# A two-layer GELU network on one core: the order of the first loads and the dummy matmuls around the first turns

## The chip, the core and the metric

The kernel runs on one core of a Trainium2 chip. The metric is the device time of one execution in microseconds; the times shown are the median of several runs.

The engines that matter here are TensorE (PE in the profile, with its weight loads PEld apart), VectorE (DVE), ScalarE (ACT), GpSimd (POOL) and SyncE (SP). Each runs its own list of instructions in order and meets the others at semaphores. SyncE, ScalarE and GpSimd also issue DMA transfers; issues appear as SPq, ACTq and POOLq.

## The reference

```python
B, S, D, F = 1, 2048, 448, 1792      # x, w1, b1, w2, b2 all bf16

def reference(x, w1, b1, w2, b2):
    h = jnp.einsum("bsd,df->bsf", x, w1) + b1
    h = _gelu(h)                      # tanh approximation
    return jnp.einsum("bsf,fd->bsd", h, w2) + b2
```

## The kernel before

The 2048 rows of x go through in four chunks of 512. For each chunk layer 1 makes h transposed (14 tiles of 128 features, by 512 rows), ScalarE applies bias and GELU on the way from PSUM to SBUF (line 284), and layer 2 multiplies by w2 and adds b2. The contraction of layer 1 is 448 long: three blocks of 128 and one of 64. Every matmul uses 64 of the array's 128 rows; matmuls come in pairs, one on each half of the rows, writing two PSUM banks, and go together. All layer matmuls are issued through `mm`, so they share line 226.

Layer 1 is written as objects `Layer1(c, j)`, j from 0 to 6, each for two feature tiles. `a` is the first half of the rows' work over the three blocks, `b_main` the second, `b_last` the 64-long rest and the activations. For the first chunk the order is by hand: the first 256 rows of x for object 0 (`L[0].a(0, HC)`), then its second 256 rows, then object 1, and so on.

x must be transposed before layer 1 can use it. For chunks 1 to 3 a DMA does it (line 151). For the first chunk TensorE does it: x's first 512 rows are loaded as they are, in two halves of 256 rows (`load_x`, line 156, events x 0 and x 1), and "turned" by transposing matmuls (`turn`, line 353): twelve for the first half, twelve for the second, and later four for the 64-wide rest (`turn_rest`). VectorE and ScalarE drain the turned blocks from PSUM (lines 364 and 366, events xT0, half, block).

Ahead of the turns TensorE runs dummies, matmuls of constant ones whose results nobody reads (`warm`, line 201): six of 512 columns and one of 128 before the first turns, one of 128 between the first and the second.

w1 is loaded in five pieces by feature tiles, cut at 0, 2, 4, 8, 12 and 14 (`load_w1`, line 134): piece 0 holds the two tiles of object 0 and has 192 KB, piece 1 those of object 1, 192 KB too, piece 2 the four tiles of objects 2 and 3. Their events are w1 0, w1 1 and so on. The last 64 rows of w1 are loaded apart in two pieces (`load_w1r`, line 141), and VectorE copies part of them to the other half of the partitions (line 420).

What sets the order of the loads is each issuing engine's list. SyncE issues x's first half, w1 piece 0, then waits at a `barrier` for the event "table", which ScalarE sets after a one-column activation that makes it load its GELU table (line 184); then come all other weights, b2, the transposing loads of x, and the stores. ScalarE issues x's second half and w1 piece 1 right at its start. GpSimd sets up the identity matrix (lines 176 and 177), sets `b2_z` to zero (line 180, event b2z0) and then issues the load of b1. The loads of these pieces have no wait of their own.

A first layer-1 matmul of object 0 waits for w1 piece 0 and for the drained block of x that it reads. A dummy waits for nothing in the kernel before; on TensorE all instructions go in the order of the list.

Of the kernel before, what the change touches and what calls it, by code (L numbers as in the profile page):

```python
# [77 lines left out]
def bass_standalone__dense_activation_gelu__prompt_kernel(  # L78
# [10 lines left out]
    P = 128  # L89
    H = P // 2  # L90
    SC = 512
    HC = SC // 2
# [9 lines left out]
    with ExitStack() as es:  # L102
# [18 lines left out]
        pr = Program(nc, es)  # L121
# [10 lines left out]
        def load_w1(i, engine="sync"):  # L132
            c0, c1 = W1CUTS[i] * P, W1CUTS[i + 1] * P
            pr.dma(engine, lambda e: e.dma_start(
                w1_sb[:, :, c0:c1], w1[0:D3, c0:c1].rearrange("(k p) f -> p k f", p=P)), ("w1", i))
# [3 lines left out]
        def load_w1r(i, engine="sync"):  # L139
            cs = slice(RCUTS[i] * P, RCUTS[i + 1] * P)  # L140
            pr.dma(engine, lambda e: e.dma_start(w1r[H:P, cs], w1[D3:D, cs]), ("w1r", i))
# [13 lines left out]
        def load_x(h, engine):  # L155
            pr.dma(engine, lambda e: e.dma_start(
                xn[:, 2 * h:2 * h + 2, :], x2[h * HC:(h + 1) * HC, :].rearrange("(p t) d -> p t d", t=2)), ("x", h))

        o0v = [out2[h * HC:(h + 1) * HC, :].rearrange("(p t) d -> p t d", t=2) for h in (0, 1)]
        load_x(0, "sync")  # L160
        load_w1(0)
        pr.barrier("sync", ["table"])
        load_w1r(0)
        load_w1(2)
        load_w1r(1)
# [5 lines left out]
        for c in range(1, NSC):  # L171
            for slot in range(KT + 1):
# [10 lines left out]
               after=["b1z"])  # L183
        pr.op("scalar", lambda e: e.activation(junk[:, :], one, ACT.Gelu_apprx_tanh), event="table")  # L184
        load_x(1, "scalar")
        load_w1(1, "scalar")

        def turn_b1():
            for q in range(4):
                pr.op("vector", lambda e, q=q: e.transpose(  # L190
                    b1t[32 * q:32 * q + 32, :], b1n[:, 32 * q:32 * q + 32]), after=["b1n"], event=("b1t", q))
            pr.op("vector", lambda e: e.tensor_copy(b1_f[:, :], b1t[:, 0:NFT]),
                  after=[("b1t", q) for q in range(4)], event="b1")
# [2 lines left out]
            pr.op("vector", lambda e: e.tensor_copy(xT[0:H, KT, s0:s1], xT[H:P, KT, s0:s1]),  # L196
                  after=after, event=event)

        def warm(n, cols=SC, u=0):
            for _ in range(n):  # L200
                pr.op("tensor", lambda e: e.matmul(unit[u][:, 0, 0:cols], lhsT=ones_w, rhs=ones_m[:, 0:cols],  # L201
                                                   start=True, stop=True))

# [150 lines left out]
        def turn_block(h, k, u, i, wait=()):  # L356
            for t in (0, 1):
                turn(lambda half, t=t: spot(u, i)[:, half, t, :], lambda rows, t=t: xn[rows, 2 * h + t, k * P:(k + 1) * P],
                     ("xt", h, k) if t else None, [("x", h)] + list(wait))
# [9 lines left out]
        def drain_block(engine, h, k, u, i, after):  # L369
            move(engine,  # L370
                 lambda t: xT[:, k, h * HC:(h + 1) * HC].bitcast(t).rearrange("p (t b s) -> p b t s", b=2, t=2),
                 lambda t: unit[u][:, :, i * H:(i + 1) * H].bitcast(t).rearrange("p b (t s) -> p b t s", t=2),
                 [after], ("xT0", h, k))
            busy[(u, 0)] = ("xT0", h, k)

        def turn_first():
            for k in (0, 2, 1):
                turn_block(0, k, k, 0)
                drain_block(("vector", "vector", "scalar")[k], 0, k, k, 0, ("xt", 0, k))
            warm(1, P, 3)  # L380
            pr.op("vector", lambda e: e.tensor_copy(
                xr[:, :, :].rearrange("p q (two h) -> p q two h", two=2),
                xn[:, :, D3:D].rearrange("p (q two) h -> p q two h", two=2)), after=[("x", 0), ("x", 1)],
                event="xr_in")
            for k in range(KT):
                turn_block(1, k, 3, k)
            for k in range(KT):
                drain_block("vector", 1, k, 3, k, ("xt", 1, 2))

        def turn_rest():  # L390


            for q in range(STC // 2):
                turn(lambda half, q=q: spot(2, 1)[:, half, q, :], lambda rows, q=q: xr[rows, q, :], ("xr", q),
                     ["xr_in", ("xT0", 0, 2)])
            for src, engine in enumerate(("vector", "scalar")):
                for dst in (src, 1 - src):
                    move(engine,
                         lambda t, src=src, dst=dst: xT[HALVES[dst], KT, 0:SC].bitcast(t).rearrange(
                             "p (q two b s) -> p b q two s", q=2, two=2, b=2)[:, :, :, src, :],  # L400
                         lambda t, src=src: unit[2][HALVES[src], :, H:2 * H].bitcast(t).rearrange(
                             "p b (q s) -> p b q s", q=2),
                         [("xr", 1)], ("xR0", dst, src))
            busy[(2, 1)] = ("xR0", 1, 0)
            busy[(2, 2)] = ("xR0", 0, 1)

        warm(NWARM)
        warm(1, P)
        turn_first()
        L = [Layer1(0, j) for j in range(NPAIR)]  # L410
        L[0].a(0, HC)
        L[0].step("a", 0, HC, SC)
        L[0].step("a", 1, HC, SC)
        turn_rest()
        L[0].step("a", 2, HC, SC)

        for i in (0, 1):
# [3 lines left out]
                  after=[("w1r", i)], event=("w1rU", i))  # L421
            if i == 0:
                turn_b1()
        L[1].a()
        L[0].b_main()
        L[1].b_main()
# [8 lines left out]
        for c in range(NSC):  # L435
# [7 lines left out]
            else:  # L443

                for row in (0, H):
                    pr.op("vector", lambda e, row=row: e.tensor_copy(b2_z[row:row + 1, :], b2_bc[row:row + 1, :]),  # L446
                          after=["b2", "b2z0"], event="b2z" if row else None)
# [59 lines left out]
```

## Time and profile before

| What | Value |
|---|---|
| Median of 5 runs | 94.37 us (93.68, 94.09, 94.37, 95.98, 96.09) |
| The profiled execution | 96.07 us; its span 94.8 us |
| PE busy | 91.5 us, 97% of the span |
| PEld busy | 51.9 us, 55% |
| ACT busy | 38.1 us, 40% |
| DVE busy | 13.8 us, 15% |
| POOL busy | 1.7 us, 2% |
| Issue of x's two halves, w1 pieces 0 and 1 | 0.75, 0.81, 1.20, 1.25 us |
| ScalarE's table ready, first SyncE issue after it | 2.25 us, 2.28 us |
| b2_z on GpSimd | 1.42 to 1.89 us |

Times within the execution are counted from its first instruction. A row of a group names the line, engine, operation, what it writes and reads, the shape and the count. In the order of time the first column is the start and the second the time from the first start to the last end of a merged run of instructions; in brackets stands how long the engine was idle before it, and what was seen to release it. Ends of matmuls are modelled, so their starts, and the starts of the weight loads, tell more than their durations. Rows of DMA issues end with the time from issue to landing.

### The profile page before, as it was taken

To read this page: it belongs to the slowest core of one execution; us is meant where nothing else is said; L and a number is where in the kernel's file an instruction comes from. 1 tells how busy PE (TensorE), PEld (TensorE's weight loads), DVE (VectorE), ACT (ScalarE), POOL (GpSimd) and SP (SyncE) were. 2 spreads that over 40 slices of the span, in tenths; PEclk is the share of its full clock that TensorE was granted. 3 is DMA by queue.
4 is the path that set the end of the run, shared out by engine and by line. 5 is a ranking of instruction groups with operands and counts; after the bars stand their busy time and mean duration, and the time that the engine had idled before them with its cause. 6 is when DMAs were issued, how large, how long until landed. Compare 5 with 4: busy or idle time off the path is not lost.

```text
span 94.8 us, 2059 instructions
## 1 busy us (share of the span) xinstructions
PE 91.5 (97%) x940; PEld 51.9 (55%) x940; DVE 13.8 (15%) x37; ACT 38.1 (40%) x63; POOL 1.7 (2%) x8
## 2 busy tenths in 40 slices
PE   6989999999999999999999999999999999999990
PEld 2464454555555444555555444555554444579990
DVE  0256002100046000000046000000044000000331
ACT  6120597830000788830000878820000878820011
POOL 6000000000000000000000000000000000000000
PEclk9999999999999999999999999999999999999999
DMA  2999999655663100000022100000021100000023
GB/s 79 320 263 330 379 282 121 120 102 111 99 107 112 49 0 7 0 0 0 0 88 64 48 0 0 3 7 0 0 96 67 37 0 0 0 0 7 0 97 97
DMA packets 13544, 7.32 MB, mean 77 GB/s; under 512 B 7264, under 2 KB 13472, under 8 KB 13536
## 3 DMA queue, kind: packets, MB, share of 16 engines
q1 hardware_dynamic: 12688, 6.70, 30.4%
q10 hardware_dynamic: 816, 0.49, 1.7%
q8 instruction: 7, 0.11, 0.5%
q14 instruction: 1, 0.01, 0.0%
q0 software_dynamic: 32, 0.00, 0.0%
HBM read 3.79 MB, written 1.84 MB: 59 GB/s over the span
## 4 chain that ended last, share of the span: by engine, by line
PE 97%; DVE 0%; ACT 0%; issue 0%
PE u L226 92%; PE u L201 3%; PE u L353 1%; DVE xT L366 0%; ACT out_sb L334 0%
## 5 line engine op out<-in xcount | busy, mean ns | idle before, releaser
L284 ACT ACTIVATE g<-u,b_f 128x512 bf16<-128x512 f32 x56 | 34.8, 685 | 41.4 <-PE u L226 41.4
L226 PE MATMUL u<-xT,w_sb 64*128 64x512 bf16 (+1 forms) x342 | 43.4, 390 | 0.4 <-DVE xT L366 0.4
L226 PE MATMUL u<-w_sb,g 64*128 64x448 bf16 (+2 forms) x504 | 43.3, 329 | 0.0
L226 PEld LDWEIGHTS u<-w_sb,g 64*128 64x128 bf16 x504 | 27.7, 94 | 15.2
L226 PEld LDWEIGHTS u<-xT,w_sb 64*128 64x128 bf16 x342 | 19.1, 98 | 19.1 <-issue 1.8
L337 DVE TENSOR_TENSOR out_sb<-u,b_bc 128x448 bf16<-128x448 f32 (+2 forms) x16 | 8.9, 591 | 64.5 <-PE u L226 64.5
L226 PE MATMUL u<-xT,w1r 64*128 64x512 bf16 x56 | 10.7, 376 | 0.0
L226 PEld LDWEIGHTS u<-xT,w1r 64*128 64x128 bf16 x56 | 3.1, 96 | 3.2 <-issue 0.4
L334 ACT CAST out_sb<-u 128x320 bf16<-128x320 f32 (+1 forms) x2 | 0.7, 345 | 8.8 <-PE u L226 8.8
L201 PE MATMUL u<-const-bfloat16-1.0 128*128 128x512 bf16 (+1 forms) x8 | 3.1, 545 | 0.8 <-PEq L492 0.8
L364 ACT COPY xT<-u 64x256 bf16<-64x256 bf16 (+1 forms) x3 | 1.1, 369 | 3.8 <-PE u L353 3.8
L366 DVE TENSOR_SCALAR xT<-u 128x128 uint32<-128x128 uint32 (+1 forms) x7 | 1.8, 285 | 4.2 <-PE u L353 4.2
L201 PEld LDWEIGHTS u<-const-bfloat16-1.0 128*128 128x128 bf16 x8 | 1.0, 134 | 2.2 <-issue 2.1
L184 ACT ACT_TABLE_LOAD x1 | 1.3, 1283 | 0.8 <-PEq L492 0.8
L446 DVE COPY b_z<-b_bc 1x448 bf16<-1x448 bf16 x2 | 0.5, 266 | 5.8 <-DMA b_bc<-in_b_dram 5.8
L196 DVE COPY xT<-xT 64x512 bf16<-64x512 bf16 x3 | 0.9, 288 | 3.1 <-DMA xT<-in_x_dram 3.1
L353 PEld LDWEIGHTS u<-ident,xn 64*128 64x128 bf16 x24 | 0.7, 121 | 0.6 <-DMA xn<-in_x_dram 0.5
L353 PE MATMUL u<-ident,xn 64*128 64x64 bf16 x24 | 1.0, 237 | 0.0
L190 DVE STREAM_TRANSPOSE b1t<-b1n 32x32 bf16<-32x32 bf16 x4 | 0.8, 202 | 0.1
L182 POOL DMA_DIRECT2D b1n<-in_b_dram x1 | 0.6, 647 | 0.0
L420 DVE COPY w1r<-w1r 64x256 bf16<-64x256 bf16 (+1 forms) x2 | 0.6, 289 | 0.4 <-DMA w1r<-in_w_dram 0.4
L180 POOL MEMSET b_z<- 128x448 bf16 x1 | 0.5, 467 | 0.0
(14 smaller groups left out, 2.7 us busy)
## 6 DMA issues: line engine op xcount, KB each, us to landing
w_sb<-in_w_dram SPq DMA_DIRECT2D x2, 784.0 KB, 8.0
out_dram<-out_sb SPq DMA_DIRECT2D x14, 112.0 KB, 1.7
w_sb<-in_w_dram SPq DMA_DIRECT2D x2, 384.0 KB, 5.4
w_sb<-in_w_dram SPq DMA_DIRECT2D x2, 192.0 KB, 4.7
xn<-in_x_dram SPq DMA_DIRECT2D x1, 224.0 KB, 2.5
xn<-in_x_dram ACTq DMA_DIRECT2D x1, 224.0 KB, 3.0
w_sb<-in_w_dram ACTq DMA_DIRECT2D x1, 192.0 KB, 4.1
xT<-in_x_dram SPq DMA_TRANSPOSE x12, 4.3
```

What stands on the lines that cost most here:

```text
L182: pr.dma("gpsimd", lambda e: e.dma_start(b1n[0:NFT, :], b1.rearrange("(c p) -> c p", p=P)), "b1n", after=["b1z"])
L184: pr.op("scalar", lambda e: e.activation(junk[:, :], one, ACT.Gelu_apprx_tanh), event="table")
L190: pr.op("vector", lambda e, q=q: e.transpose(b1t[32 * q:32 * q + 32, :], b1n[:, 32 * q:32 * q + 32]), after=["b1n"], event=("b1t", q))
L196: pr.op("vector", lambda e: e.tensor_copy(xT[0:H, KT, s0:s1], xT[H:P, KT, s0:s1]), after=after, event=event)
L201: pr.op("tensor", lambda e: e.matmul(unit[u][:, 0, 0:cols], lhsT=ones_w, rhs=ones_m[:, 0:cols], start=True, stop=True))
L226: o = pr.op("tensor", lambda e: e.matmul(unit[u][:, lo, cols], lhsT=lhsT, rhs=rhs, start=start, stop=stop, skip_group_check=skip), after=a ...
L284: pr.op("scalar", lambda e, lo=lo, ft=ft: e.activation(g[:, ft, c * SC:(c + 1) * SC], unit[u][:, lo, :], ACT.Gelu_apprx_tanh, bias=b1_f[:, ...
L334: pr.op("scalar", lambda e, j=j: e.copy(out_sb[:, j, d0:d1], unit[u][:, 1, 0:d1 - d0]), after=[("y", j, d0)], event=("o", j, d0))
L337: pr.op("vector", lambda e, j=j, lo=lo: e.tensor_tensor(out=out_sb[:, j, d0:d1], in0=unit[u][:, lo, 0:d1 - d0], in1=b2_bc[:, d0:d1], op=AL ...
L353: pr.op("tensor", lambda e, half=half, rows=rows: e.transpose(o(half), i(rows), ident[rows, rows]), after=after + ["ident"], event=event i ...
L364: pr.op(engine, lambda e: e.copy(out(BF16), in_(BF16)), after=after, event=event)
L366: pr.op(engine, lambda e: e.tensor_single_scalar(out(U32), in_(U32), 0, ALU.bitwise_or), after=after, event=event)
```

## The change

The first pieces of w1 change places: piece 0 is now issued by ScalarE, behind x's second half, and piece 1 by SyncE. SyncE's wait stands ahead of piece 1 now, and is for b2_z's zeros on GpSimd in place of ScalarE's table. The dummy ahead of the first turns and the one between the turns grow from 128 to 256 columns. A third dummy of 256 columns is put behind the second turns; it waits for the first drained block of x, and the layer-1 matmuls come after it. The lists of ScalarE, GpSimd and VectorE are otherwise the same.

```diff
         load_x(0, "sync")
-        load_w1(0)
-        pr.barrier("sync", ["table"])
+        pr.barrier("sync", ["b2z0"])
+        load_w1(1)
         load_w1r(0)
         load_w1(2)
...
         load_x(1, "scalar")
-        load_w1(1, "scalar")
+        load_w1(0, "scalar")
...
-        def warm(n, cols=SC, u=0):
+        def warm(n, cols=SC, u=0, after=()):
             for _ in range(n):
                 pr.op("tensor", lambda e: e.matmul(unit[u][:, 0, 0:cols], lhsT=ones_w, rhs=ones_m[:, 0:cols],
-                                                   start=True, stop=True))
+                                                   start=True, stop=True), after=after)
...
                 turn_block(0, k, k, 0)
                 drain_block(("vector", "vector", "scalar")[k], 0, k, k, 0, ("xt", 0, k))
-            warm(1, P, 3)
+            warm(1, HC, 3)
...
         warm(NWARM)
-        warm(1, P)
+        warm(1, HC)
         turn_first()
+        warm(1, HC, 0, [("xT0", 0, 0)])
         L = [Layer1(0, j) for j in range(NPAIR)]
         L[0].a(0, HC)
```

## The prediction

> **What bounds the kernel now.** I read the chain of waits first. It is TensorE work nearly from end to end:
>
> ```profile
> 4.72 0.02 issue
> 4.74 0.30 DVE xT L366
> 5.04 0.01 issue
> 5.05 1.25 PE u L226 x10
> 6.30 0.11 PE u L353 x4
> 6.41 86.24 PE u L226 x891
> ```
>
> After 5.05 us TensorE never stops, so the end can move only by (a) when that stream starts and (b) how fast its matmuls go. Fewer bytes or faster engines elsewhere are worth nothing.
>
> For (b) I put two stretches of the layer-1 matmuls side by side, 6.3 to 9.7 us and 10.4 to 14 us (columns: count, then minimum/median/maximum ns of one):
>
> ```profile
> L226 PE MATMUL u<-xT,w_sb x19: 398/631/632, 5.9 to 9.4; 64*128 64x512 bf16 x16, 64*128 64x256 bf16 x3
> ...
> L226 PE MATMUL u<-xT,w_sb x30: 376/376/377, 10.6 to 13.8; 64*128 64x512 bf16 x30
> ```
>
> The same form takes 631 ns early and 376 ns late. Those are latencies; the rate is in the weight loads between, from the order of time:
>
> ```profile
> 9.38 0.17 PEld L226 LDWEIGHTS u<-xT,w_sb 64*128 64x128 bf16 x2 [0.25 <-issue]
> 9.81 0.17 PEld L226 LDWEIGHTS u<-xT,w1r 64*128 64x128 bf16 x2 [0.25 <-issue]
> ...
> 10.13 0.11 PEld L226 LDWEIGHTS u<-xT,w1r 64*128 64x128 bf16 x2 [0.15 <-issue]
> 10.35 0.11 PEld L226 LDWEIGHTS u<-xT,w_sb 64*128 64x128 bf16 x2
> ```
>
> A pair of loads serves a pair of 512-column matmuls, one in each half of the rows, that run together. The step is 0.43 us (9.38 to 9.81), then 0.32, then 0.22. So TensorE ran at half rate until W = 10.03 us: the step of 0.32 is 0.22 us at half and 0.10 at full rate, and 9.81 + 0.22 = 10.03. The page's clock row shows 9 tenths all along and can't be used for this. Every us of dense work before W costs half a us.
>
> For (a), the order of time ahead of the stream:
>
> ```profile
> 0.79 2.83 PE L201 MATMUL u<-const-bfloat16-1.0 128*128 128x512 bf16 x7 [0.79 <-PEq L492]
> 3.54 0.50 PE L353 MATMUL u<-ident,xn 64*128 64x64 bf16 x12
> 3.98 0.29 PE L201 MATMUL u<-const-bfloat16-1.0 128*128 128x128 bf16 x1
> 4.20 0.50 PE L353 MATMUL u<-ident,xn 64*128 64x64 bf16 x12
> 5.05 1.25 PE L226 MATMUL u<-xT,w_sb 64*128 64x256 bf16 x10 [0.35 <-DVE xT L366]
> ```
>
> TensorE idles for 0.35 us before the stream. The releaser named, a DVE drain of x's second half, is not needed by the first matmul, whose own drain (the first on DVE, from 3.87) was long done. It also needs w1's first tiles, and these are the late ones:
>
> ```profile
> xn<-in_x_dram SPq DMA_DIRECT2D x1, 224.0 KB, 2.5
> xn<-in_x_dram ACTq DMA_DIRECT2D x1, 224.0 KB, 3.0
> w_sb<-in_w_dram SPq DMA_DIRECT2D x1, 192.0 KB, 3.7
> w_sb<-in_w_dram ACTq DMA_DIRECT2D x1, 192.0 KB, 4.1
> ```
>
> Issued at 0.75, 0.81, 1.20 and 1.25, they land at 3.2, 3.8, 4.9 and 5.3 us.
>
> [...]
>
> [...] The profiled execution took 96.07 us (span 94.8 and 1.27 around it), 1.7 above the median of 94.37. Of the five runs, two (95.98, 96.09) look like the profiled one, and three (93.68, 94.09, 94.37) like runs that switched earlier: (96.07 - 94.37) x 2 = 3.4 us earlier, so at 6.6, and 5.25 for the fastest. These are estimates, since only one trace is there.
>
> **The change, part by part.**
>
> *Longer dummies before and between the turns.* 128 columns more each, at half rate 0.427 x 128 / 512 = 0.107 us each. Neither is covered: x's first half landed at 3.2 and the turns start at 3.54, when the dummies are through; the second landed at 3.8, before the turns at 4.20. So 0.21 us on TensorE's path, less up to 0.03 at the first.
>
> *The new dummy after the turns.* It waits for the first drain on DVE, done by 4.17, before TensorE gets there, so the wait costs nothing. 256 columns are 0.21 us; changing from turns to a dummy and back costs as the middle dummy does: turns through at about 3.86, next at 4.20, that is 0.34 with 0.107 of columns, so 0.23 of change. Sum 0.44 us. Behind it on TensorE stands the whole stream. The second turns, through at about 4.51, are now through at 4.71; plus 0.44 is 5.15. The stream starts at **5.15 for 5.05: +0.10 us**, with the idle 0.35 us as cover for the rest.
>
> *w1's first tiles (event w1 0) on ScalarE's queue.* Issued at 1.25 in place of 1.20, behind x's second half (3.8). *Its next tiles (w1 1)* leave SyncE once b2_z's memset on GpSimd ends (1.42 + 0.47 = 1.89), so about 1.91 in place of 1.25. That takes 192 KB from beside the first tiles for some 0.6 us. At the 309 KB/us and more of 2 to 4 us, the first tiles should land 0.2 to 0.5 us earlier, 4.4 to 4.7; bounds: 4.2 and, if the order in the queue hurts, 5.5. Worth nothing by itself while the dummies run to 5.15, but it makes the start TensorE's own. The next tiles land later, 5.4 to 5.9 for 5.3. They are needed after six pairs of 256 columns and four turns: 6 x 0.21 + 0.1 = 1.4 us past the start at half rate, 0.75 at full rate, so at 5.9 or later: nothing, but nothing to spare.
>
> *All later loads on SyncE.* The old wait ended at 2.25 with the table; now one issue (0.42) and a gap come after 1.91, so the rest is issued 0.15 to 0.2 us later: w1r's first part (landed 5.7; its copy on DVE starts only at 7.08), w1's 384 KB tiles (landed 8.0, to 8.2), all else. In the trace these have slack; at full rate from the start, the 384 KB tiles are wanted after those six pairs and 11 pairs of 512 columns (11 x 0.216 = 2.4), at about 5.15 + 0.75 + 2.4 = 8.3: no loss counted, up to 0.3 us possible. GpSimd and ScalarE issue the same things in the same order: nothing.
>
> [...] TensorE is now busy from 0.79 on but for the changes of mode, with 0.43 us more dummy columns around the turns[...] the fastest run before already suggests 5.25. I take 4.7[...]. Saving (10.03 - 4.7) / 2 = 2.67; cost 0.10, half of it if the clock is up by then: 96.07 - 2.67 + 0.05 = **93.4 us**. Bounds: W at 3.5 gives 92.8; 6.6 gives 94.4.
>
> **Rivals.**
>
> [...] (0.17). Short gaps don't decide, or the dummies are too few. Then the time is the median plus 0.10: 94.5. For it: three runs of five were quick without the change. Against: two were not[...].
>
> *The first tiles come later[...]* (0.23; slower). [...] If they land where the next tiles do now, at 5.33, the stream starts at 5.45: +0.4 us of idle beside the new dummy, which gives back the 0.43 of new columns, so nearly every run switches at about 10: 96.07 + 0.1 to 0.2 = 96.2. It decides from a landing past 5.15. Against it: the next tiles are issued 0.66 us later than the first.
>
> *The hold does nothing*: the next tiles' data begins when it did, since a transfer's data starts well after its issue (nothing moves before 1.8 us). Then landings stay near 4.9, still before 5.15, and the main case holds; its price is none.
>
> **How the numbers follow.** Main case 0.60, its own range 92.7 to 94.4; [...] 0.45 faster by over 1% (below 93.43), 0.15 within. No effect: 0.12 within, 0.03 faster, 0.02 slower. Late tiles: 0.23 slower. One per cent is about what a measurement of this kernel can tell from no change. Faster 0.48, same 0.27, slower 0.25. The range must reach into the slow case: 92.7 to 96.1.
>
> **What would show it.** Right: no idle time before the first L226 matmul, which starts at 5.1 to 5.2; the first tiles landed by 4.7; three L201 dummies of 256 columns; steps of 0.22 us between weight loads from about 5 us. Wrong: W still near 10; or a landing past 5.15 with idle time before the stream. [...]

## The result and the profile after

| | before | changed |
|---|---|---|
| Median of all runs | 94.00 us (93.30 to 96.35, 79 runs) | 94.17 us (93.59 to 96.05, 44 runs) |
| Runs at 95.4 us or more | 29 of 79 | 2 of 44 |
| Mean of all runs | 94.55 us | 94.24 us |
| The other runs: mean, first and last tenth | 93.81; 93.51, 94.17 | 94.16; 93.82, 94.48 |
| Ratio to before | | 1.0037, interval 1.0024 to 1.0050 |

The ratio leaves out runs more than 1.5% above the quickest of their kernel, which here are those in which TensorE's clock rises late (95.4 us or more, the late runs of what follows). So the change is 0.4% slower in the ratio, and it does something else that the ratio can't show: the gap between 94.6 and 95.4, in which no run of this table lies, is crossed by far fewer runs.

The profiled execution of the changed kernel (96.05 us, span 94.7) has the late clock, as that of before had, so the two can be laid side by side. The chain of waits (start, length, what):

```profile
0.74 0.46 ACT L184
1.20 0.03 issue
1.22 4.33 DMA w_sb<-in_w_dram
5.56 0.05 issue
5.61 1.25 PE u L226 x7
6.85 0.11 PE u L353 x4
6.96 85.65 PE u L226 x702
```

Before, the chain ran through TensorE's dummies and turns to a stream that starts at 5.05. Now its head is a transfer: piece 0 of w1, issued by ScalarE at 1.22, which lands 4.33 us later. The stream starts at 5.61. TensorE's own order of time (start, length, engine, line, shape, count, and in brackets the idle time ahead and its releaser):

```profile
3.65 0.50 PE L353 MATMUL u<-ident,xn 64*128 64x64 bf16 x12
4.08 0.40 PE L201 MATMUL u<-const-bfloat16-1.0 128*128 128x256 bf16 x1
4.41 0.50 PE L353 MATMUL u<-ident,xn 64*128 64x64 bf16 x12
4.84 0.40 PE L201 MATMUL u<-const-bfloat16-1.0 128*128 128x256 bf16 x1
5.61 0.39 PE L226 MATMUL u<-xT,w_sb 64*128 64x256 bf16 x2 [0.37 <-DMA w_sb<-in_w_dram]
```

The turns and dummies are where the prediction put them (turns at 3.65 for 3.54 and 4.41 for 4.20, third dummy at 4.84), but 0.37 us of idle time is still there. The issues and their time to landing:

```profile
xn<-in_x_dram SPq DMA_DIRECT2D x1, 224.0 KB, 2.6
xn<-in_x_dram ACTq DMA_DIRECT2D x1, 224.0 KB, 3.0
w_sb<-in_w_dram ACTq DMA_DIRECT2D x1, 192.0 KB, 4.3
w_sb<-in_w_dram SPq DMA_DIRECT2D x1, 192.0 KB, 4.0
```

Piece 0 takes 4.3 us where it took 3.7, and lands at 5.56. Piece 1, issued at 1.91, takes 4.0 and lands at 5.88, where it was at 5.33. The rate, from the weight loads:

```profile
8.68 0.15 PEld L226 LDWEIGHTS u<-xT,w_sb 64*128 64x128 bf16 x2 [0.28 <-issue]
9.10 0.15 PEld L226 LDWEIGHTS u<-xT,w_sb 64*128 64x128 bf16 x2 [0.28 <-issue]
9.47 0.31 PEld L226 LDWEIGHTS u<-xT,w_sb 64*128 64x128 bf16 x4 [0.22 <-issue]
```

The steps are 0.42, then 0.37, after which four loads come in 0.31. The step of 0.37 is 0.30 us at half and 0.07 at full rate, so the clock rises at 9.10 + 0.30 = 9.40 us, against 10.03 before. That gain of 0.63 us is worth 0.31, and the start 0.56 us later, in a stretch at half rate, costs 0.28. The spans are 94.7 and 94.8. Here the two nearly cancel. Most runs of the changed kernel are not like this one, and what sets their time took the experiments to see.

### The profile page after: what moved, and what is told of

Read it like the earlier page. It is cut to its first block, busy times and chain, and to the rows that moved or that the text cites. A ratio compares the mean times of both kernels' runs of the same rounds, so it can differ in the third digit from the quotient of the medians.

```text
span 94.7 us, 2060 instructions
## 1 busy us (share of the span) xinstructions
PE 91.4 (97%) x941; PEld 46.3 (49%) x941; DVE 13.8 (15%) x37; ACT 38.2 (40%) x63; POOL 1.7 (2%) x8
## 4 chain that ended last, share of the span: by engine, by line
PE 92%; DMA 5%; ACT 1%; issue 0%
PE u L226 92%; DMA w_sb<-in_w_dram 5%; ACT L184 0%; ACT out_sb L334 0%; PE u L353 0%
## 5 line engine op out<-in xcount | busy, mean ns | idle before, releaser
L226 PE MATMUL u<-xT,w_sb 64*128 64x512 bf16 (+1 forms) x342 | 42.5, 386 | 0.4 <-DMA w_sb<-in_w_dram 0.4
L226 PEld LDWEIGHTS u<-w_sb,g 64*128 64x128 bf16 x504 | 25.0, 94 | 17.8
L226 PEld LDWEIGHTS u<-xT,w_sb 64*128 64x128 bf16 x342 | 16.5, 97 | 21.5 <-issue 1.6
L201 PE MATMUL u<-const-bfloat16-1.0 128*128 128x512 bf16 (+1 forms) x9 | 3.7, 552 | 0.8 <-PEq L493 0.8
L226 PEld LDWEIGHTS u<-xT,w1r 64*128 64x128 bf16 x56 | 2.6, 94 | 3.4
```

What stands on the lines that cost most here:

```text
L226: o = pr.op("tensor", lambda e: e.matmul(unit[u][:, lo, cols], lhsT=lhsT, rhs=rhs, start=start, stop=stop, skip_group_check=skip), after=a ...
```

## The experiments

**The first four** take the change apart. The theories named in the expectations: A, the order of loads costs and the dummies help the clock; B, the loads cost nothing and the dummies cost; C, the ratio above 1 is only the mix of runs.

The order of loads alone, with the dummies of before:

```diff
         load_x(0, "sync")
-        load_w1(0)
-        pr.barrier("sync", ["table"])
+        pr.barrier("sync", ["b2z0"])
+        load_w1(1)
...
-        load_w1(1, "scalar")
+        load_w1(0, "scalar")
```

> The changed order of loads alone (w1 piece 0 on ScalarE behind x's second half, piece 1 on SyncE behind the zeros), with the dummies of the kernel before. Theory A (the loads cost, the dummies help the clock): the first layer-1 matmul starts up to 0.5 us later than 5.05, and with the idle gap longer the clock rises late (times of 95.4 and more) in as many runs as before or more, over 35%; the other runs are 0.2 to 0.5 us above those of before, ratio 1.003 to 1.005. Theory B (the loads cost nothing, the dummies cost): ratio 0.999 to 1.001.

Measured: ratio 1.0028 (0.9998 to 1.0058), span 93.1; 1 of 14 runs late. The size fits A, though the interval just reaches 1; the place does not fit: piece 0 landed at 4.68 and the stream started at 4.81, earlier than before. The loss is further on:

```profile
4.81 1.25 PE L226 MATMUL u<-xT,w_sb 64*128 64x256 bf16 x10
5.83 0.34 PE L353 MATMUL u<-ident,xr 64*128 64x64 bf16 x4
5.96 0.34 PE L226 MATMUL u<-xT,w_sb 64*128 64x256 bf16 x2
6.57 0.60 PE L226 MATMUL u<-xT,w_sb 64*128 64x512 bf16 x4 [0.27 <-DMA w_sb<-in_w_dram]
```

This is TensorE in order of time. The first object's last pair is at 5.96, and the second object, whose matmuls have 512 columns, starts at 6.57, released by a transfer: piece 1, which landed at 6.53. And the clock rose early nearly always (24 of 67 runs of the kernel before were late beside it), though no dummy was added. With piece 0 there sooner, no idle time is listed ahead of the stream (0.35 us in the profile before); that this is the reason is not shown.

The dummies alone, with the loads of before:

```diff
-            warm(1, P, 3)
+            warm(1, HC, 3)
...
-        warm(1, P)
+        warm(1, HC)
         turn_first()
+        warm(1, HC, 0, [("xT0", 0, 0)])
```

> The three dummies alone, with the order of loads of before. Theory A: the late rise of the clock all but goes (under 10% of the runs at 95.4 or more), the stream starts at 5.15 to 5.2 in place of 5.05, other runs at 93.9 to 94.0, ratio 1.001 to 1.002. Theory B: the ratio is that of the whole change, 1.003 to 1.005. Theory C (the ratio above 1 is only that runs which were late before now sit at the upper end of the quick ones): the quickest tenth is where it was before, 93.5, and the slowest tenth of the quick runs moves from 94.2 to 94.5.

Measured: median 93.81 beside 94.01 of before, ratio 1.0001 (0.9978 to 1.0025), span 92.1; 0 of 22 late. B falls here; a repeat below has 1.0022. The first tenth of the runs is at 93.54 and the last at 94.44, as C has it for these dummies. In the changed kernel C is not enough: there both tenths lie 0.31 us higher than before (93.51 and 94.17, 93.82 and 94.48). The profile has full rate from the start of the stream and no wait at the second object (5.47 is the first object's last pair, the second follows at 5.59):

```profile
4.62 0.28 PE L201 MATMUL u<-const-bfloat16-1.0 128*128 128x256 bf16 x1
4.84 0.72 PE L226 MATMUL u<-xT,w_sb 64*128 64x256 bf16 x10
5.40 0.22 PE L353 MATMUL u<-ident,xr 64*128 64x64 bf16 x4
5.47 1.15 PE L226 MATMUL u<-xT,w_sb 64*128 64x256 bf16 x10
```

All dummies, piece 0 back on SyncE, piece 1 behind the zeros on SyncE too:

```diff
         load_x(0, "sync")
+        load_w1(0)
         pr.barrier("sync", ["b2z0"])
         load_w1(1)
...
-        load_w1(0, "scalar")
```

> All dummies of the change, but w1 piece 0 stays on SyncE right behind x's first half; piece 1 follows on SyncE after the zeros, and ScalarE issues only x's second half. Theory A, if it is the place behind x's second half in ScalarE's queue that delays piece 0: it lands by 4.6, the stream starts at 5.15, ratio 1.000 to 1.002. If it is the late piece 1 and its followers that get in the way, as in the change: 1.003 to 1.005.

Measured: ratio 1.0042 (1.0026 to 1.0058), span 92.8; 0 of 22 late. Piece 0 landed at 4.75 and the stream started at 4.92; piece 1 landed at 6.11. The weight loads show the wait (0.50 us of idle time):

```profile
5.56 0.10 PEld L226 LDWEIGHTS u<-xT,w_sb 64*128 64x128 bf16 x2
6.16 0.33 PEld L226 LDWEIGHTS u<-xT,w_sb 64*128 64x128 bf16 x6 [0.50 <-DMA w_sb<-in_w_dram]
```

So ScalarE's queue is not needed for the loss; the hold of piece 1 is enough.

The change without its third dummy (its line taken out):

> The change without its third dummy. If the third dummy is what the clock needs: late rises come back, over 20% of the runs at 95.4 or more. If it is on the path of the quick runs: these gain 0.1 to 0.3 us over the change, ratio about 1.001; if the landing of w1 piece 0 sets the start anyway, they stay at 94.15, ratio 1.003 to 1.004.

Measured: ratio 1.0024 (1.0005 to 1.0043), span 93.0; 0 of 22 late, though one run, at 95.22, lies between the two groups and is not in the ratio. The late rises did not come back, against what I expected of the third dummy. Piece 0 landed at 4.74, piece 1 at 6.34, and the second object started at 6.39: the quick runs stay where they were (median 94.16).

**The next four** test the hold from the other side, and the dummies.

The change with piece 1 on SyncE right behind x's first half:

```diff
-        pr.barrier("sync", ["b2z0"])
         load_w1(1)
+        pr.barrier("sync", ["table"])
```

> The change without its hold: w1 piece 0 on ScalarE behind x's second half, piece 1 on SyncE right behind x's first half at 1.2 us, SyncE's wait for the table after it as before; all three dummies. If the hold is the cause (piece 1 lands at 6.1 to 6.5 and TensorE waits for it at the second object): piece 1 lands by 5.6, no idle time there, quick runs as with the dummies alone, ratio 0.999 to 1.001. If the place of piece 0 behind x's second half is the cause: piece 0 lands past 5.1, ratio 1.003 or more.

Measured: ratio 1.0047 (1.0029 to 1.0065), span 92.9; 3 of 7 late. The hold is gone, piece 1 landed at 5.08, and it is no better: now piece 0 is the last of the four and landed at 5.56:

```profile
4.65 0.28 PE L201 MATMUL u<-const-bfloat16-1.0 128*128 128x256 bf16 x1
5.61 0.72 PE L226 MATMUL u<-xT,w_sb 64*128 64x256 bf16 x10 [0.67 <-DMA w_sb<-in_w_dram]
```

The idle time ahead of the stream is longer than before (0.67 us for 0.35), and late rises are back in spite of all the dummies, though of seven runs only. My first theory held the hold alone to blame; without it the ratio is no lower (1.0047, and 1.0048 for the change in the same batch), with the wait at piece 0 in place of piece 1.

The two longer dummies without the third, loads of before:

> Loads of the kernel before, the two longer dummies, no third. If length ahead of and between the turns is enough for the clock: under 10% of the runs at 95.4 or more. If the gap after the second turns decides: about as many as before, over 25%. Quick runs 0 to 0.1 us under those with the third, ratio 0.999 to 1.000.

Measured: 4 of 22 late (12 of 30 of the kernel before beside it), ratio 1.0024 (1.0007 to 1.0041), between the two answers that I had given for the late runs; the quick runs are not quicker than with the third dummy.

The change once more, for a profile with the early clock:

> The change once more, for the profile of an execution whose clock rises early. If the wait is for piece 1: the stream starts at 4.8 to 5.0, piece 1 lands at 6.1 to 6.5, TensorE waits for it from about 5.7 and loses 0.4 to 0.7 us there; span 92.6 to 93.0 against 92.1 with the dummies alone; ratio 1.003 to 1.005. If piece 0 is what is late, as in the profile with the late clock: the stream starts past 5.3.

Measured: ratio 1.0048 (1.0030 to 1.0066), span 93.2; 0 of 7 late. Piece 0 landed at 4.69, piece 1 at 6.46. The expected wait is not there:

```profile
5.18 1.25 PE L226 MATMUL u<-xT,w_sb 64*128 64x256 bf16 x10
6.22 0.32 PE L353 MATMUL u<-ident,xr 64*128 64x64 bf16 x4
6.34 0.86 PE L226 MATMUL u<-xT,w_sb 64*128 64x256 bf16 x6
```

In this execution the first object ran at half rate (ten matmuls in 1.25 us, against 0.72 with the dummies alone) and TensorE reached the second at 6.54 (6.34 is the first object's last pair), just after piece 1 had landed. A clock that rose sooner could not have started it before 6.5.

Pieces 0 and 1 each cut in two by partitions, halves on both queues, no hold; loads else as before, all dummies:

```diff
-        load_w1(0)
+        load_w1_half(0, 0, "sync")
+        load_w1_half(1, 0, "sync")
...
-        load_w1(1, "scalar")
+        load_w1_half(0, 1, "scalar")
+        load_w1_half(1, 1, "scalar")
```

> All dummies; w1 pieces 0 and 1 each cut in two by partitions, one half on SyncE and one on ScalarE, piece 0 ahead of piece 1 on both, no hold. If the start of the stream waits for piece 0 with the dummies alone (it landed at 4.79 and the stream began at 4.84): piece 0 lands 0.1 to 0.3 earlier, and the quick runs gain up to 0.2 us, ratio 0.997 to 0.999. If TensorE's own string of turns and dummies sets the start, or the smaller transfers take longer: 1.000 to 1.002.

Measured: ratio 1.0074 (1.0050 to 1.0099), 3 of 6 late, the stream at 5.78 in the profile. A miss: of the 32 parts that piece 0 now has, 22 had landed by 4.75, but the last landed at 5.74.

**The next four.** All dummies, both pieces on ScalarE behind x's second half:

```diff
-        pr.barrier("sync", ["b2z0"])
-        load_w1(1)
+        pr.barrier("sync", ["table"])
...
         load_w1(0, "scalar")
+        load_w1(1, "scalar")
```

> All dummies; ScalarE issues x's second half, w1 piece 0 and piece 1, one behind the other; SyncE waits for the table as before and goes on with w1r. If the hold of piece 1 behind the zeros is what the change pays for: piece 1 is issued at 1.7 in place of 1.9 and has SyncE's queue beside it empty until 2.3, lands by 5.7, no wait at the second object, ratio 0.999 to 1.001. If any order that puts piece 1 behind the other three costs as much: it lands past 6.0, ratio 1.003 to 1.005. Late rises of the clock under 10% in both, since piece 0 lands by 4.8.

Measured: ratio 1.0058 (1.0034 to 1.0081), 7 of 16 at 95.38 or more. Issued at 1.71, piece 1 landed at 7.55 in the profile, and TensorE idled 1.8 us at the second object; these runs are spread up to 98.85. So an issue 0.2 us earlier than in the change brought a landing 1.1 us later, with SyncE's transfers beside it.

The profiled execution (96.96 us) is not one with a late rise. Its first object went at full rate (ten matmuls in 0.73 us from 4.85 on), and after the idle time the weight loads come 0.43 us apart: the clock had fallen back. Here the profile's own row of the granted clock shows it, in slices of 2.39 us (mean over the span 0.982):

```profile
PEclk9995799999999999999999999999999999999999
```

In finer slices it is 0.61 from 7 to 8 us, 0.50 from 8 to 10 and 0.68 from 10 to 11, so it fell at about 7.2 and rose at 10.6. From the second object to the end 88.1 us pass where other kernels with the early clock need 86.6 (table below): the wait cost another 1.5 us after it was over.

The kernel before without its two short dummies (lines 380 and 408):

> The kernel before without the two dummies of 128 columns (six of 512 stay). [...] If the dummies around the turns don't matter: about as many as before, a third. The stream's start stays at 4.9 to 5.1, where piece 0 lands; quick runs within 0.1 us of before.

Measured: 7 of 14 late, ratio 0.9998 (0.9980 to 1.0016). Beside it the kernel before had 28 late runs of 61, nearly the same share, so these runs don't show that the two short dummies do anything. The profile is of an execution with the early clock (93.92 us, span 92.6):

```profile
3.75 0.35 PE L353 MATMUL u<-ident,xn 64*128 64x64 bf16 x12 [0.25 <-DMA xn<-in_x_dram]
5.31 0.72 PE L226 MATMUL u<-xT,w_sb 64*128 64x256 bf16 x10 [0.70 <-DMA w_sb<-in_w_dram]
```

The first twelve turns take 0.35 us, where they took 0.50 in the profile before: the clock is up by 3.75. Then TensorE stands for 0.70 us until piece 0 has landed, at 5.17.

The third dummy alone, on the kernel before:

> Loads and short dummies of the kernel before, with the third dummy alone added. If filling the gap after the second turns is what the clock needs: late rises in under 10% of the runs; ratio of the quick runs 1.000 to 1.001, since the dummy ends by 5.0, before piece 0 has landed. If the sum of columns counts: between the kernel before (a third) and the two longer dummies (4 of 22).

Measured: 3 of 22 late (28 of 61 of the kernel before beside it), ratio 1.0001 (0.9980 to 1.0022).

The three dummies with the loads of before, again:

> The three dummies with the loads of before once more, as the best version so far: under 10% late rises, median 0.2 us or more below that of before, ratio of the quick runs 0.998 to 1.002; in the profile no wait for piece 1 at the second object.

Measured: median 94.03 beside 94.15, ratio 1.0022 (1.0002 to 1.0041), span 92.7; 0 of 22 late. The median gained 0.12 us, not 0.2. Piece 0 landed at 5.36 in this profile, with 0.4 us of idle time ahead of the stream.

That a run of 95.4 us or more has the late clock is read from the profiles: in three of 96.05 to 96.12 us the rate doubles at 9.4 to 10.0, in the twelve of 93.45 to 94.55 us by 6.7. The exception is the one above whose clock fell back.

The share of late runs differs from batch to batch in the kernel before itself, from 24 of 67 to 13 of 26, so each count has to be read beside its own batch. With the loads of before, and the kernel before in brackets: none 7 of 14 (28 of 61), the longer two 4 of 22 (12 of 30), the short two and the third 3 of 22 (28 of 61), all three 0 of 44 (52 of 128). The last two are clear of the kernel before; the first two are not.

**The last two** ask why a held piece 1 lands so late. In the change, and in the dummies alone, SyncE is held until x's second half is there before it issues w1r and the rest. In the dummies alone this wait takes the place of the one for the table; in the change it comes on top, behind piece 1:

```diff
         load_w1(1)
+        pr.barrier("sync", [("x", 1)])
         load_w1r(0)
```

> The change, with SyncE held once more after piece 1, until x's second half has landed (about 3.8 to 4.2 us), before w1r and all that follows. If the followers' traffic makes piece 1 late: it lands by 5.6, no wait at the second object, ratio 0.999 to 1.001. If its late issue does: it still lands past 5.9, ratio 1.002 to 1.005. The 384 KB piece lands some 0.5 us later than in the change and is wanted at about 8.5 to 9: at most 0.2 us lost there.

> The three dummies with the loads of before, but SyncE's wait ahead of w1r is for x's second half in place of the table, so 1.6 us longer. If the followers' traffic counts: pieces 0 and 1 land 0.1 to 0.4 us earlier (before 4.8 and 5.3), the second object starts at 5.6 to 5.8 and the ratio is 0.997 to 0.999, with no late rise of the clock: better than both kernels. If it doesn't: 1.000 to 1.002. If the followers then come too late themselves, TensorE waits for the 384 KB piece at about 8 us: 1.001 to 1.004.

Measured: ratios 1.0088 (1.0056 to 1.0121) and 1.0062 (1.0037 to 1.0087). Of the 17 runs of the first, one took 95.61 us and one 535.32 us, which has no explanation and is not in the ratio; of the 10 of the second none was late. In the change piece 1 landed at 5.71, though issued at 1.91, and with the dummies alone at 5.11; the second object started at 6.04 and 5.71 with no wait. In the five profiles with the hold and the followers right behind, piece 1 had landed at 5.88 to 6.53. So traffic of the followers is what makes a held piece 1 late, as far as one profile each can show it. But the wait has only moved. From the second of these, weight loads in order of time:

```profile
7.43 0.31 PEld L226 LDWEIGHTS u<-xT,w1r 64*128 64x128 bf16 x4
8.60 0.33 PEld L226 LDWEIGHTS u<-xT,w_sb 64*128 64x128 bf16 x6 [0.85 <-DMA w_sb<-in_w_dram]
```

After the rests of the first two objects TensorE now waits for piece 2, the 384 KB for objects 2 and 3, which landed at 8.56; with the dummies alone and no such hold it landed at 7.7. The loss is bigger than the one removed.

The profiles with the early clock can be summed up by one number. When the second object starts, nearly all that is left is TensorE's stream at full rate:

| Kernel | piece 0 landed | piece 1 landed | stream | second object | span | span less second object |
|---|---|---|---|---|---|---|
| dummies alone | 4.79 | 5.52 | 4.84 | 5.59 | 92.1 | 86.5 |
| kernel before without its short dummies | 5.17 | 5.71 | 5.31 | 6.02 | 92.6 | 86.6 |
| third dummy alone | 5.14 | 5.62 | 5.19 | 5.91 | 92.5 | 86.6 |
| dummies alone, again | 5.36 | 5.60 | 5.41 | 6.13 | 92.7 | 86.6 |
| hold on SyncE | 4.75 | 6.11 | 4.92 | 6.16 | 92.8 | 86.6 |
| two longer dummies | 5.06 | 5.47 | 5.19 | 6.42 | 93.0 | 86.6 |
| change without hold | 5.56 | 5.08 | 5.61 | 6.33 | 92.9 | 86.6 |
| change without third dummy | 4.74 | 6.34 | 4.88 | 6.39 | 93.0 | 86.6 |
| change, loads alone | 4.68 | 6.53 | 4.81 | 6.57 | 93.1 | 86.5 |
| change | 4.69 | 6.46 | 5.18 | 6.54 | 93.2 | 86.7 |
| dummies alone, followers held | 4.94 | 5.11 | 4.98 | 5.71 | 92.8 | 87.1 |
| change, followers held | 4.66 | 5.71 | 5.17 | 6.04 | 93.2 | 87.2 |

The last column is the same to 0.2 us, but for the last two rows, which have their wait later, at piece 2. The second object starts when piece 1 is there and TensorE is through with the first object. With the two longer dummies it was the latter: piece 1 was there at 5.47, but the first object went at half rate. And the two profiles of the dummies alone lie 0.54 us apart in it (5.59 and 6.13), so one profile of each kernel does not measure a difference of a few tenths; the ratios do.

## Why the prediction was wrong

*What bounds the kernel*: right as far as it went. All of it lies before the stream is in full flow, and the clock rose at an early or a late time. But the saving was counted from the profiled execution, with W (the time at which the rate doubles) at 10.03, as if TensorE were held up by its clock alone down to W = 4.7. That is the step that failed first: "Saving (10.03 - 4.7) / 2 = 2.67". The 4.7 was my estimate, shown by no trace of the kernel before, and the 2.67 was counted from an execution with the late clock, and the median run is not one: the kernel before had its clock up early in 50 of 79 runs already (mean 93.81), and its median, 94.00, is among these. The 29 late runs have a mean of 95.83, so the two groups are 2.0 us apart, not 2.67. Nor are the runs with the three dummies (means 93.87 and 94.08) quicker than the quick runs of the kernel before beside them (93.85 and 93.89). No profile of a quick run of before was taken; in the nearest one, without the short dummies, the clock is up by 3.75 and the landing of piece 0 sets the start, at 93.92 us in all. The forecast is what single executions reach (93.45 with the dummies alone, where piece 0 landed at 4.79; 93.30 before the change), not what most do. (Its own sum, 96.07 - 2.67 + 0.05, is 93.45 and not 93.4.)

*When the rate doubles (W)*: right in the effect of the dummies on the late runs, which all but go. With the loads of before the three dummies had no late rise in 44 runs, where the kernel before had 52 in 128 beside them, and the change has 2 of 44 (29 of 79). What makes the clock rise early or late is not shown. These runs don't settle whether idle time decides: the counts fall with the three dummies, but taking out the short two changed nothing that 14 runs can show, and the change without its hold and the cut pieces had 3 of 7 and 3 of 6 late runs with all three dummies in. W was put at 4.7; in one execution without the short dummies the clock was up by 3.75. The mean of all runs did fall, by 0.3 us; the forecast was 1.0 us off the median of 94.37.

*w1's next tiles (piece 1)*: wrong in size, and this is what raised the ratio. "The next tiles land later, 5.4 to 5.9 for 5.3 ... nothing, but nothing to spare." In the four profiles with the hold and the early clock it landed at 6.1 to 6.5 (5.88 in the one with the late clock). w1r and piece 2 are issued right behind it; with these held back it landed at 5.71, in one profile. I had priced the bandwidth for the pieces ahead and not for those behind. In three of the four TensorE stood at the second object until piece 1 came. What was costed at nothing is 0.57 us in the starts of the second object between one profile of the dummies alone and that of the hold on SyncE (5.59 and 6.16), and 0.36 us in the means of their runs (93.87 and 94.24, 22 runs each side by side). Not all of the 0.35 us by which the quick runs of the change are slower need be the loads: the dummies alone have ratios of 1.0001 and 1.0022, and how much of the second is their own cost, and how much the mix of runs of theory C, stays open.

*w1's first tiles (piece 0)*: the band of 4.4 to 4.7 fits the change with the early clock (4.69) and the loads alone (4.68); in the profiled execution of the change it was 5.56, past the bound of 5.5.

*The dummies on TensorE's path*: right. The stream starts at 5.18 in the change with the early clock (5.15 forecast), with piece 0 there since 4.69. That the third dummy makes the quick runs slower is not shown (ratios 1.0037 with it and 1.0024 without, intervals overlap).

*The rivals*: "Short gaps don't decide, or the dummies are too few" came nearest, with 94.5 for 94.17, and by luck: the late runs all but went (2 of 44 for 29 of 79), and it was the quick runs that lost 0.35 us. The slower case came true to the letter in the profiled execution (piece 0 at 5.56, past 5.15, idle time behind the new dummy, 96.05 us for 96.2), but only 2 of 44 runs are that slow. In the others it is right in kind, a new wait for a landing, and has the wrong piece. "The hold does nothing" falls: held, piece 1 landed at 5.9 to 6.5, and at 5.3 to 5.7 where it left early with the loads of before.

*Later loads*: "no loss counted, up to 0.3 us possible" at piece 2 holds for the change. The last two runs show what lies behind it: 1.6 us more delay cost 0.5 to 0.6 us there (87.1 and 87.2 in the table for 86.6).

The dummies without the new order of loads is the best version found: no late rises in 44 runs, mean 93.87 and 94.08 against 94.58 and 94.76 of before beside it. Without the late runs its ratio is 1.0001 and 1.0022, the second clear of 1 by a hair, so it isn't quicker in the usual run.

## What to carry to other kernels

Where the times of a kernel fall into two groups, find out which group the profiled execution belongs to before counting a saving from it; a cure for the rarer group moves a mean and hardly a median. When a stretch waits for one load after another, write down for each piece when it lands and when it is wanted, for all pieces, and with what the ones issued behind it do to it: here the held piece 1 landed at 6.46 with the others right behind it and at 5.71 with these held back. A hold that brings one forward can make the next one the wait, as here piece 0 at 4.69 and piece 1 at 6.46. And compare counts of slow runs only with those of the same batch.

## What the runs showed that was not expected

In the profiled execution of the change the semaphore of piece 0 was stepped 16 times: 14 by 4.39 us, the others at 5.12 and 5.56. The stream, which starts at 5.61, waited for the one straggler. In the execution with the early clock all 16 came from 4.29 to 4.69.

Piece 1 as third on ScalarE's queue was such a case too. Issued at 1.71, it had 15 of its 16 steps by 6.40, and the last came at 7.55. Its place in the queue is then not all: an estimate without the straggler is a wait of 0.7 us at the second object (from 5.77, where the first ends, to 6.45), in place of 1.8. Why one part of 16 comes so late stays open.

In the same execution the wait was paid for twice. TensorE had stood still for about 1.4 us when its clock fell back to half, and it stayed there for 3.4 us.
